# Attention and a gated feed-forward on one core: the value product on 128 rows in every pass, and the statistics of q and k in a PSUM bank of VectorE's own

## The chip, the core and the metric

The kernel runs on one core of a Trainium2 chip. The core has five engines with their own instruction streams: TensorE (PE in the profile; PEld is its weight load), VectorE (DVE), ScalarE (ACT), GpSimd (POOL) and SyncE (SP, here only a DMA queue). On-chip memory is SBUF (128 partitions, read and written by all engines and by DMA) and PSUM (8 banks of 128 x 512 float32), into which TensorE writes. The metric is the device time of one execution in microseconds (us), as the median of some runs; lower is better.

## The reference

```python
def rmsnorm(x, g):
    return x / np.sqrt(np.mean(x * x, axis=-1, keepdims=True) + 1e-06) * g
# q, k, v: 8 batches, 12 heads, 448 tokens, 64 features, float32
q_n, k_n = rmsnorm(q, g_q), rmsnorm(k, g_k)
scores = (1.0 / np.sqrt(64)) * np.matmul(q_n, k_n.transpose(0, 1, 3, 2))
attn = softmax(scores)                     # with 1e-09 added to the sum
x = np.matmul(attn, v)                     # -> [8, 448, 768]
x_prev = x shifted by one token
xk = mu_k * x + (1.0 - mu_k) * x_prev
xr = mu_r * x + (1.0 - mu_r) * x_prev
k = np.maximum(xk @ w_k, 0.0)              # 768 -> 1024; the weights are float64
out = sigmoid(xr @ w_r) * (k * k @ w_v)    # 1024 -> 768
```

## The kernel before

Every float32 product is made of float16 parts: a value is split into a high and a low half ("hi", "lo"), and three products (hi hi, hi lo, lo hi) are added up in PSUM.

Attention goes over 48 **pairs** of heads (`i`), and its inputs over 24 **quads** of heads (`u`, two pairs each).

- `prep(u)` normalises k and q of a quad. ScalarE squares (`xs`), GpSimd adds halves of the squares (L167), VectorE sums them (L170) into 28 numbers a partition, two short VectorE instructions scale them (L172, L173), and `rsqrt` (L64) takes the reciprocal root by a bit trick (L67, L68) and three Newton steps of three instructions each (L70, L71, L72). All of it lies in SBUF: the statistics and the root in a tile `ss` of 56 columns, the scratch in a tile that the profile calls `rs`. GpSimd multiplies q and k by the root (L179), ScalarE and GpSimd split them (L184, L186), and DMA transposes on SyncE's queue put them into `stk`.
- `vprep(i)` scales v of a pair. Each row's sum of squares is spread over the partitions by a small matmul (L204) into a PSUM tile `tr`, VectorE takes its maximum (L206) and makes a power of two of it (L208 to L210), ScalarE writes the high half `vh` (L211), VectorE the low half `vl` (L215).
- `group_scores` makes scores of 64 to 128 query rows (TensorE, L235), their maxima (VectorE, L258) and their exponentials in place in PSUM (ScalarE, L259). `group_probs` divides by the sum (L271, L272), splits the result (ScalarE L277, VectorE L278: tile `ph`), and a DMA transpose on SyncE's queue makes `pT`.
- `attend(i)` multiplies `pT` with `vh` and `vl` in 11 passes over the same PSUM tile `av`, two matmuls (one per head) in a pass. A pass takes 128 rows of `pT`; ten of them use all, and the eighth, `(1, 3, HD)`, only the first 64, so that its matmuls have the tile shape 64*64 on the array where the others have 128*64. ScalarE then scales `av` into `x` (L303).

`weight_tile` turns the float64 weights into scaled float16 halves in 20 tiles: VectorE assembles float32 (L404 to L406, two rounds a tile), six or eight matmuls write a Gram matrix into the PSUM tile `av` (L412), VectorE multiplies it by the identity (L416), a matmul sums it (L417), VectorE takes the maximum (L418). `moe(b)` is the feed-forward of a batch, with its matmuls at L456 into the PSUM tile `mm`.

The eight PSUM banks are: `sc` four, `mm` two, `av` one (attention's value product and the weights' Gram matrices by turns), `tr` one (`vprep` and the one call of `allmax`). A tile with one buffer is given to its next user when the last one's reader is done; the users have the order in which the code asks for it.

The three streams (attention, weights, feed-forward) are interleaved by the loop at the end of the kernel, and a scheduler then sets the order in which each engine's instructions stand. Each engine works its instructions off in that order and stands still when the first of them waits.

Of the kernel before, what the change touches and what calls it, by code (L numbers as in the profile page):

```python
# [7 lines left out]
F32 = mybir.dt.float32  # L8
F16 = mybir.dt.float16
BF16 = mybir.dt.bfloat16  # L10
I32 = mybir.dt.int32
AF = mybir.ActivationFunctionType
ALU = mybir.AluOpType
AX = mybir.AxisListType

P = 128
HD = 64
NT = 7
# [36 lines left out]
def spread(ap, n):  # L55
    return bass.AP(tensor=ap.tensor, offset=ap.offset, ap=[list(x) for x in ap.ap] + [[0, n]])
# [4 lines left out]
    return bass.AP(tensor=ap.tensor, offset=ap.offset + off, ap=[list(ap.ap[0]), [HD, 2], [2 * HD, NT], [1, HD]])  # L61


def rsqrt(nc, pool, y, a, n, tag):  # L64
    t = pool.tile([P, n], F32, name=tag)
    yi = y.bitcast(I32)
    nc.vector.tensor_scalar(out=yi, in0=a.bitcast(I32), scalar1=1, scalar2=None, op0=ALU.logical_shift_right)  # L67
    nc.vector.tensor_scalar(out=yi, in0=yi, scalar1=-1.0, scalar2=float(0x5F3759DF), op0=ALU.mult, op1=ALU.add)  # L68
    for _ in range(NEWTON):
        nc.vector.tensor_tensor(out=t, in0=y, in1=y, op=ALU.mult)  # L70
        nc.vector.scalar_tensor_tensor(out=t, in0=t, scalar=-0.5, in1=a, op0=ALU.mult, op1=ALU.mult)  # L71
        nc.vector.scalar_tensor_tensor(out=y, in0=t, scalar=1.5, in1=y, op0=ALU.add, op1=ALU.mult)  # L72


def attn_moe_kernel(tc, q, k, v, g_q, g_k, mu_k, mu_r, w_k, w_v, w_r, out):
    nc = tc.nc
# [11 lines left out]
    ident16 = const.tile([P, P], BF16, name="ident16")  # L88
    nc.scalar.copy(out=ident16, in_=ident)

    def allmax(src, n, r):
        pt = ps.tile([P, 512], F32, name="tr", bufs=1)
        nc.tensor.transpose(out=pt[0:n, 0:P], in_=src, identity=ident)
        m = small.tile([P, 1], F32, name="allmax")
        nc.vector.tensor_reduce(out=m[0:n, :], in_=pt[0:n, 0:P], axis=AX.X, op=ALU.max)
        nc.tensor.matmul(out=pt[:, P:P + n], lhsT=m[0:n, :].broadcast_to([n, P]), rhs=ident[0:n, 0:n], start=True, stop=True)
        nc.vector.tensor_copy(out=r, in_=pt[:, P:P + n])
# [13 lines left out]
    gm = const.tile([P, 8], F32, name="gm")  # L111
    nc.vector.tensor_reduce(out=gm[:, 0:1], in_=G, axis=AX.X, op=ALU.max, apply_absolute_value=True)
    nc.vector.tensor_scalar(out=gm[:, 0:1], in0=gm[:, 0:1], scalar1=TINY, scalar2=None, op0=ALU.max)
    rsqrt(nc, small, gm[:, 1:2], gm[:, 0:1], 1, "rs1")
    nc.vector.tensor_scalar(out=G, in0=G, scalar1=gm[:, 1:2], scalar2=None, op0=ALU.mult)
    nc.vector.tensor_tensor(out=gm[:, 2:3], in0=gm[:, 1:2], in1=gm[:, 1:2], op=ALU.mult)
    nc.vector.tensor_scalar(out=gm[:, 3:4], in0=gm[:, 2:3], scalar1=1.0 / HD, scalar2=None, op0=ALU.mult)
# [21 lines left out]
    NSS = 4 * NT  # L139
# [19 lines left out]
        VF[i] = vf  # L159

    def prep(u):
        ss = small.tile([P, 2 * NSS], F32, name="ss", bufs=2)
        for n, t in enumerate(LD[u]):
            tv = t.rearrange("p h (t d) -> p (h t) d", d=HD)
            xs = ap_.tile([P, 2 * NT, HD], F32, name="xs", bufs=1)
            nc.scalar.activation(out=xs, in_=tv, func=AF.Square)  # L166
            nc.gpsimd.tensor_tensor(out=xs[:, :, 0:HD // 2], in0=xs[:, :, 0:HD // 2], in1=xs[:, :, HD // 2:], op=ALU.add)  # L167
            if n == 0:
                nc.gpsimd.tensor_tensor(out=tv, in0=tv, in1=bcast(G[:, :], 2 * NT), op=ALU.mult)  # L169
            nc.vector.tensor_reduce(out=ss[:, 2 * NT * n:2 * NT * (n + 1)], in_=xs[:, :, 0:HD // 2], axis=AX.X, op=ALU.add)  # L170
            yield
        nc.vector.tensor_scalar(out=ss[:, 0:2 * NT], in0=ss[:, 0:2 * NT], scalar1=1.0 / HD, scalar2=1e-6, op0=ALU.mult, op1=ALU.add)  # L172
        nc.vector.tensor_scalar(out=ss[:, 2 * NT:NSS], in0=ss[:, 2 * NT:NSS], scalar1=gm[:, 3:4], scalar2=gm[:, 4:5], op0=ALU.mult, op1=ALU.add)  # L173
        rsqrt(nc, small, ss[:, NSS:2 * NSS], ss[:, 0:NSS], NSS, "rs28")
        yield
        T = [ap_.tile([P, 2, 2 * NT, HD], F16, name="stk", bufs=3) for x in range(2)]
        for n, t in enumerate(LD.pop(u)):
            tv = t.rearrange("p h (t d) -> p (h t) d", d=HD)
            nc.gpsimd.tensor_tensor(out=tv, in0=tv, in1=spread(ss[:, NSS + 2 * NT * n:NSS + 2 * NT * (n + 1)], HD), op=ALU.mult)  # L179
            pool = pro[0] if u < NP // 2 and n else ap_  # L180
            nat = pool.tile([P, 2 * NT, P], F16, name="nat", bufs=1)
            hi, lo = heads(nat, 0), heads(nat, NT * P)
            t4 = t.rearrange("p h (t d) -> p h t d", d=HD)
            nc.scalar.copy(out=hi, in_=t4)  # L184
            yield
            nc.gpsimd.tensor_tensor(out=lo, in0=t4, in1=hi, op=ALU.subtract)  # L186
            for x in range(2):
                nc.sync.dma_start_transpose(out=T[x][:, n], in_=nat[x * HD:(x + 1) * HD].rearrange("p a c -> p (a c)"))
            yield
        for x in range(2):  # L190
            TQ[2 * u + x] = T[x]

    def vprep(i):
# [5 lines left out]
        vh = ap_.tile([P, 2, NT, HD], F16, name="vh", bufs=2)  # L199
        vl = ap_.tile([P, 2, 4, HD], F16, name="vl", bufs=2)  # L200
        vs = small.tile([P, 2], F32, name="vs", bufs=2)
        pt = ps.tile([P, 512], F32, name="tr", bufs=1)
        nc.scalar.activation(out=vh[0:HD].rearrange("p h t d -> p h (t d)").bitcast(BF16), in_=vf[0:HD], func=AF.Square, accum_out=vs[0:HD, 0:1])
        nc.tensor.matmul(out=pt[:, 0:HD], lhsT=vs[0:HD, 0:1].bitcast(BF16)[:, 1:2].broadcast_to([HD, P]), rhs=ident16[0:HD, 0:HD], start=True, stop=True)  # L204
        yield
# [78 lines left out]
                nc.sync.dma_start_transpose(out=pT[:, h, :, t0 * HD:], in_=ph[h * HD:(h + 1) * HD, 0, :])  # L284
        yield

    PASSES = [(hl, c, P) for c in range(3) for hl in range(2)] + [(0, 3, P), (1, 3, HD)] + [(0, c, P) for c in range(4, 7)]

    def attend(i):
        vh, vl, iv = VV.pop(i)  # L290
# [319 lines left out]
```

## Time and profile before

| | us |
|---|---|
| median of 3 runs (lowest, highest) | 1267.06 (1266.27, 1267.16) |
| the profiled execution, its own time | 1263.01 |
| span of its instructions | 1261.2 |
| TensorE matmul busy | 1017.4 |
| VectorE busy | 901.4 |
| ScalarE busy | 794.4 |
| GpSimd busy | 681.4 |
| mean granted TensorE clock | 0.911 |

Busy time is the union of an engine's instructions. A line of the page names the source line, the engine, the operation, the tile written and those read (`ss<-rs,ss`), the shapes, the count, and then busy time in us and the mean of one in ns. Where a tile's or a line's instructions are listed, the three numbers are the shortest, median and longest duration in ns. A view of windows gives each engine's busy time in a stretch of the span, with the number of instructions. A view of waits says which engine's instruction stood idle until which other one, with the sum in us, the number of times and the longest.

The span has three stages: up to about 400 us the weights are prepared beside the first twelve or so pairs; up to 1174 us attention and feed-forward run beside each other; then the rest of the feed-forward runs alone.

### The profile page before, as it was taken

The page shows a single profiled execution, that of the slowest core. Times are in us where ns is not written, and L with a number is a line of the kernel's source. Part 1 is how long each engine was busy: PE and PEld are TensorE (multiplying, and loading weights), DVE is VectorE, ACT ScalarE, POOL GpSimd, SP SyncE. Part 2 cuts the span into 40 slices and gives each one's busy share as a digit, 9 for nine tenths or more (in the row PEclk, how much of TensorE's full clock was granted, in tenths as well). Part 3 has the DMA queues.
Part 4 walks back from the last instruction along what each step waited for, and adds up shares of the span by engine and source line. Part 5 has one row for each costly group of instructions (what it writes and reads, how often), then busy time and mean ns, then how long its engine had stood idle before and what let it go on. Part 6 is the DMA issues. An engine that isn't in the chain of part 4 may idle for free. (4 is left out here: it accounts for less than half of the span.)

```text
span 1261.2 us, 18897 instructions
## 1 busy us (share of the span) xinstructions
PE 1017.4 (81%) x5935; PEld 471.4 (37%) x5935; DVE 901.4 (71%) x2356; ACT 794.4 (63%) x1756; POOL 681.4 (54%) x678
## 2 busy tenths in 40 slices
PE   1125545586799999889999899898989999999998
PEld 0002222233244344433443444344434444344454
DVE  5886899979967868675786667776887687667200
ACT  3266656566756777577676765776778676876311
POOL 2642465736655657375467536674568455523731
PEclk9956656588799999998999999999989999999999
DMA  7589977978586878768777676978986787776101
GB/s 161 119 152 168 178 155 160 172 153 165 110 148 134 146 145 167 139 131 142 143 147 147 128 138 138 167 132 152 167 162 129 151 150 125 136 144 102 26 13 38
DMA packets 456356, 172.77 MB, mean 137 GB/s; under 512 B 411200, under 2 KB 452672, under 8 KB 456256
## 3 DMA queue, kind: packets, MB, share of 16 engines
q1 hardware_dynamic: 423328, 132.24, 59.2%
q10 hardware_dynamic: 32928, 39.34, 12.8%
q8 instruction: 46, 0.75, 0.2%
q14 instruction: 54, 0.44, 0.1%
HBM read 61.41 MB, written 11.01 MB: 57 GB/s over the span
## 5 line engine op out<-in xcount | busy, mean ns | idle before, releaser
L278 DVE SCALAR_TENSOR_TENSOR ph<-sc,sums,ph 128x448 f16<-128x448 f32 x322 | 210.0, 676 | 87.8 <-ACT ph L277 87.2
L259 ACT ACTIVATE sc<-sc,sums 128x448 f32<-128x448 f32 x322 | 193.3, 612 | 108.8 <-DVE sums L258 91.5
L235 PE MATMUL sc<-stk 64*128 64x448 f16 (+1 forms) x1104 | 189.9, 379 | 68.1 <-DVE ph L278 49.7
L456 PE MATMUL mm<-wvh,kk 128*128 128x384 f16 x896 | 234.6, 330 | 0.1
L456 PE MATMUL mm<-xk,wkh 128*128 128x448 f16 x768 | 220.9, 366 | 12.7 <-ACT kf L478 6.0
L277 ACT ACTIVATE ph<-sc,sums 128x448 f16<-128x448 f32 x322 | 189.6, 645 | 50.3 <-DMA pT<-ph 15.7
L258 DVE TENSOR_REDUCE sums<-sc 128x1 f32<-128x448 f32 x322 | 187.8, 613 | 22.8 <-PE sc L235 22.3
L456 PE MATMUL mm<-wrh,xr 128*128 128x384 f16 x672 | 178.4, 329 | 6.9 <-ACT th L512 4.7
L235 PE MATMUL av<-pT,vh 128*64 128x448 f16 x672 | 142.0, 389 | 40.8 <-DMA pT<-ph 26.0
L456 PEld LDWEIGHTS <-kk 128*128 128x128 f16 x1344 | 125.8, 98 | 101.0 <-issue 25.3
L456 PE MATMUL mm<-wvl,kk 128*128 128x384 f16 x448 | 147.5, 329 | 0.0
L456 PE MATMUL mm<-xk,wkl 128*128 128x448 f16 x384 | 140.6, 366 | 0.0
L186 POOL TENSOR_TENSOR nat<-qk,nat 128x896 f16<-128x896 f32 x48 | 91.2, 1900 | 74.4 <-ACT nat L184 74.3
L167 POOL TENSOR_TENSOR xs<-xs 128x448 f32<-128x448 f32 x48 | 56.2, 1172 | 138.1 <-ACT xs L166 138.0
L235 PEld LDWEIGHTS <-stk 64*128 64x128 f16 (+1 forms) x1152 | 57.6, 101 | 193.5 <-issue 142.3
L456 PEld LDWEIGHTS <-xr 128*128 128x128 f16 x1008 | 93.1, 98 | 85.1 <-issue 23.6
L373 DVE SCALAR_TENSOR_TENSOR df<-x,bsc,df 128x448 f32<-128x448 f32 x90 | 90.7, 1018 | 35.8 <-POOL df L372 35.6
L179 POOL TENSOR_TENSOR qk<-qk,ss 128x896 f32<-128x896 f32 x48 | 82.0, 1728 | 60.2 <-DVE ss L72 49.2
L456 PE MATMUL mm<-wrl,xr 128*128 128x384 f16 x336 | 110.5, 329 | 0.0
L456 PEld LDWEIGHTS <-wkh 128*128 128x128 f16 x768 | 72.8, 100 | 92.8 <-issue 39.0
L516 POOL TENSOR_TENSOR o<-th,bsc 128x384 f32<-128x384 f32 x48 | 43.2, 899 | 104.8 <-DVE th L515 68.1
L166 ACT ACTIVATE xs<-qk 128x896 f32<-128x896 f32 x48 | 45.8, 954 | 79.3 <-DMA qk<-in_q_dram 50.8
(124 smaller groups left out, 1722.2 us busy)
## 6 DMA issues: line engine op xcount, KB each, us to landing
vf<-in_v_dram SPq DMA_DIRECT2D x48, 224.0 KB, 3.8
qk<-in_k_dram ACTq DMA_DIRECT2D x48, 224.0 KB, 4.9
qk<-in_q_dram ACTq DMA_DIRECT2D x48, 224.0 KB, 4.8
out_dram<-o SPq DMA_DIRECT2D x56, 192.0 KB, 2.9
vf<-in_v_dram SPq DMA_DIRECT2D x48, 192.0 KB, 3.8
raw<-in_moe_w_k_dram ACTq DMA_DIRECT2D x16, 384.0 KB, 3.9
raw<-in_moe_w_v_dram ACTq DMA_DIRECT2D x12, 512.0 KB, 4.7
raw<-in_moe_w_r_dram ACTq DMA_DIRECT2D x12, 384.0 KB, 4.5
```

The source lines that it names most:

```text
L166: nc.scalar.activation(out=xs, in_=tv, func=AF.Square)
L167: nc.gpsimd.tensor_tensor(out=xs[:, :, 0:HD // 2], in0=xs[:, :, 0:HD // 2], in1=xs[:, :, HD // 2:], op=ALU.add)
L179: nc.gpsimd.tensor_tensor(out=tv, in0=tv, in1=spread(ss[:, NSS + 2 * NT * n:NSS + 2 * NT * (n + 1)], HD), op=ALU.mult)
L186: nc.gpsimd.tensor_tensor(out=lo, in0=t4, in1=hi, op=ALU.subtract)
L235: return op(**kw)
L258: nc.vector.tensor_reduce(out=sums[:, t:t + 1], in_=sp[:, 0:S], axis=AX.X, op=ALU.max, negate=True)
L259: nc.scalar.activation(out=sp[:, 0:S], in_=sp[:, 0:S], func=AF.Exp, bias=sums[:, t:t + 1], accum_out=sp[:, S:S + 1])
L277: nc.scalar.activation(out=ph[:, j, 0:S], in_=sp[:, 0:S], func=AF.Copy, scale=r[:, j:j + 1])
L278: nc.vector.scalar_tensor_tensor(out=ph[:, j, S:], in0=sp[:, 0:S], scalar=r[:, j:j + 1], in1=ph[:, j, 0:S], op0=ALU.mult, op1=ALU.subtract)
L373: nc.vector.scalar_tensor_tensor(out=df, in0=xc, scalar=sc[:, MX + j:MX + j + 1], in1=df, op0=ALU.mult, op1=ALU.add)
L456: nc.tensor.matmul(out=ps_, lhsT=la(i, a), rhs=ra(i, c), start=(i == 0 and a + c == 0), stop=(i == n - 1 and a == 1))
L516: nc.gpsimd.tensor_tensor(out=o[:, hs].rearrange("p (c n) -> p c n", n=P), in0=th.rearrange("p (c n) -> p c n", n=P), in1=spread(rsu[:, ND ...
```

## The change

It has two parts, and one that follows from the second.

1. In `PASSES` the eighth pass takes all 128 rows: `(1, 3, P)`. The second 64 rows add, for every seventh token, the low half of its probabilities times the low half of its values, a term that was left out before. All 22 matmuls of a pair now have the shape 128*64.
2. A PSUM tile `misc` is allotted once for the whole program. The statistics of q and k and the scratch of `rsqrt` lie in it, in 56 columns for even quads and 56 for odd ones, and only VectorE touches it. The root itself stays in SBUF (tile `ss`, now 28 columns), since GpSimd reads it. `rsqrt` is rewritten so that each of its instructions with two tensors takes one from `misc` and one from SBUF; it has as many instructions as before. In the setup one copy of a column into `misc` is added.
3. `misc` takes the bank of `tr`, so the PSUM tile of `vprep` and of `allmax` becomes a user of the bank `av`.

```diff
-def rsqrt(nc, pool, y, a, n, tag):
-    t = pool.tile([P, n], F32, name=tag)
-    yi = y.bitcast(I32)
-    nc.vector.tensor_scalar(out=yi, in0=a.bitcast(I32), scalar1=1, scalar2=None, op0=ALU.logical_shift_right)
-    nc.vector.tensor_scalar(out=yi, in0=yi, scalar1=-1.0, scalar2=float(0x5F3759DF), op0=ALU.mult, op1=ALU.add)
+def rsqrt(nc, y, a, t):
+    ti = t.bitcast(I32)
+    nc.vector.tensor_scalar(out=ti, in0=a.bitcast(I32), scalar1=1, scalar2=None, op0=ALU.logical_shift_right)
+    nc.vector.tensor_scalar(out=y.bitcast(I32), in0=ti, scalar1=-1.0, scalar2=float(0x5F3759DF), op0=ALU.mult, op1=ALU.add)
     for _ in range(NEWTON):
-        nc.vector.tensor_tensor(out=t, in0=y, in1=y, op=ALU.mult)
-        nc.vector.scalar_tensor_tensor(out=t, in0=t, scalar=-0.5, in1=a, op0=ALU.mult, op1=ALU.mult)
+        nc.vector.tensor_tensor(out=t, in0=a, in1=y, op=ALU.mult)
+        nc.vector.scalar_tensor_tensor(out=t, in0=t, scalar=-0.5, in1=y, op0=ALU.mult, op1=ALU.mult)
         nc.vector.scalar_tensor_tensor(out=y, in0=t, scalar=1.5, in1=y, op0=ALU.add, op1=ALU.mult)
...
+    misc = ps.tile([P, 512], F32, name="misc", bufs=1)
+
     def allmax(src, n, r):
-        pt = ps.tile([P, 512], F32, name="tr", bufs=1)
+        pt = ps.tile([P, 512], F32, name="av", bufs=1)
...
-    rsqrt(nc, small, gm[:, 1:2], gm[:, 0:1], 1, "rs1")
+    nc.vector.tensor_copy(out=misc[:, 510:511], in_=gm[:, 0:1])
+    rsqrt(nc, gm[:, 1:2], misc[:, 510:511], misc[:, 511:512])
...
     def prep(u):
-        ss = small.tile([P, 2 * NSS], F32, name="ss", bufs=2)
+        y = small.tile([P, NSS], F32, name="ss", bufs=2)
+        o = (u % 2) * 2 * NSS
+        ss, tm = misc[:, o:o + NSS], misc[:, o + NSS:o + 2 * NSS]
...
-        rsqrt(nc, small, ss[:, NSS:2 * NSS], ss[:, 0:NSS], NSS, "rs28")
+        rsqrt(nc, y, ss, tm)
...
-            nc.gpsimd.tensor_tensor(out=tv, in0=tv, in1=spread(ss[:, NSS + 2 * NT * n:NSS + 2 * NT * (n + 1)], HD), op=ALU.mult)
+            nc.gpsimd.tensor_tensor(out=tv, in0=tv, in1=spread(y[:, 2 * NT * n:2 * NT * (n + 1)], HD), op=ALU.mult)
...
     def vprep(i):
-        pt = ps.tile([P, 512], F32, name="tr", bufs=1)
+        pt = ps.tile([P, 512], F32, name="av", bufs=1)
...
-    PASSES = [(hl, c, P) for c in range(3) for hl in range(2)] + [(0, 3, P), (1, 3, HD)] + [(0, c, P) for c in range(4, 7)]
+    PASSES = [(hl, c, P) for c in range(3) for hl in range(2)] + [(0, 3, P), (1, 3, P)] + [(0, c, P) for c in range(4, 7)]
```

The kernel's line numbers grow by one to four below the first of these lines; L67 to L72 of before are L66 to L71 after, L204 is L208, L412 is L416, L417 is L421.

The scheduler's order changes in many small places on every engine; the numbers of instructions stay, but for the one copy on VectorE. Two places show what matters. The first is VectorE in `prep` of one quad: what its instructions of the reciprocal root write and read (the first Newton step and its start). Before:

```order
L173 TENSOR_SCALAR ss<-ss,gm 128x14 [waits DVE_49]
L67 TENSOR_SCALAR ss<-ss 128x28 [waits DVE_49]
L68 TENSOR_SCALAR ss<-ss 128x28 [waits DVE_49]
L70 TENSOR_TENSOR rs_3281<-ss 128x28 [waits DVE_49]
L71 SCALAR_TENSOR_TENSOR rs_3281<-rs_3281,ss 128x28 [waits DVE_49]
L72 SCALAR_TENSOR_TENSOR ss<-rs_3281,ss 128x28 [waits DVE_49]
```

After (other instructions of VectorE stand between some of these, in both):

```order
L177 TENSOR_SCALAR misc<-misc,gm 128x14 [waits DVE_49]
L66 TENSOR_SCALAR misc<-misc 128x28 [waits DVE_49]
L67 TENSOR_SCALAR ss<-misc 128x28 [waits DVE_49]
L69 TENSOR_TENSOR misc<-misc,ss 128x28 [waits DVE_49]
L70 SCALAR_TENSOR_TENSOR misc<-misc,ss 128x28 [waits DVE_49]
L71 SCALAR_TENSOR_TENSOR ss<-misc,ss 128x28 [waits DVE_49]
```

All of them still wait only for VectorE itself; of the two tensors that one reads, one now is in PSUM (`misc`).

The second is TensorE among the weights: the matmul of `vprep` (`vs` is its stationary input) beside the Gram matrices (`wf`) and their sum (`dg`) of the fourth and fifth weight tile. Before, it has a bank of its own and stands ahead of the sum, with nothing to wait for but its input:

```order
L235 LDWEIGHTS stk [waits DMAHW1_49,DMAHW3_49]
L235 MATMUL sc<-stk 128x448 [waits DVE_49]
L204 LDWEIGHTS vs [waits Activation_49]
L204 MATMUL tr<-ident_75,vs 128x64
L417 MATMUL av<-dg,ones 128x128 [waits DVE_49]
L412 LDWEIGHTS wf
L412 MATMUL av<-wf 128x128 [waits DVE_49]
```

After, it stands between the sum of one tile and the Gram matrix of the next:

```order
L421 MATMUL av<-dg,ones 128x128 [waits DVE_49]
L208 LDWEIGHTS vs [waits Activation_49]
L208 MATMUL av<-ident_75,vs 128x64 [waits DVE_49]
L416 LDWEIGHTS wf
L416 MATMUL av<-wf 128x128 [waits DVE_49]
```

It moved behind the sum, now waits for VectorE to have read that sum, and the next Gram matrix waits for VectorE to have read its result.

## The prediction

> **What bounds the kernel now.** I read the windows of the three stages first, then what TensorE and VectorE wait for in each, then the rows of the instructions that change.
>
> Busy times of the three stages (stretch, its length, then busy time and count of PE, PEld, DVE, ACT, POOL; clock, DMA share, GB/s):
>
> ```profile
> 0.00:400.00 400.00, 217.94 (x1164) 96.11 (x1165) 326.29 (x846) 232.18 (x479) 206.87 (x182) 0.76 0.79 152
> 400.00:1174.00 774.00, 719.52 (x4308) 329.89 (x4305) 563.07 (x1495) 541.21 (x1230) 439.42 (x458) 0.98 0.76 142
> 1174.00:1261.20 87.20, 79.90 (x467) 45.39 (x465) 12.07 (x15) 21.03 (x48) 35.08 (x39) 0.98 0.07 19
> ```
>
> The first 400 us are VectorE's: it is busy for 82% of them (326 of 400), TensorE for 54%. In the next 774 us TensorE is busy for 93% (54.5 us idle) and VectorE for 73%. The last 87 us are feed-forward alone, nearly all TensorE. A microsecond saved is thus worth most on VectorE in the first stage and on TensorE in the second.
>
> TensorE's waits, from 0 to 400 us:
>
> ```profile
> PE av L412 <- DVE wf L406: 40.4, 12, 7.8
> PE sc L235 <- DVE ph L278: 32.0, 11, 15.2
> ...
> PE av L235 <- DVE WSC L418: 6.2, 4, 3.4
> PE av L412 <- DVE WSC L418: 6.1, 3, 3.4
> ```
>
> From 400 to 1174 us:
>
> ```profile
> PE av L235 <- DMA pT<-ph: 26.0, 22, 3.0
> PE sc L235 <- DVE ph L278: 17.7, 18, 2.5
> ```
>
> And VectorE's own longest there:
>
> ```profile
> DVE ph L278 <- ACT ph L277: 69.6, 63, 4.2
> ```
>
> Early on TensorE waits for VectorE by name; later its idle time goes first to the transposes of the probabilities, then to VectorE (17.7 us), and VectorE itself waits for ScalarE. So what VectorE gains later reaches the end only in part.
>
> **The short instructions of `prep` (term 1).** These are the instructions on the tile `ss` (shortest, median and longest in ns), then their busy time by stage:
>
> ```profile
> L70 DVE TENSOR_TENSOR rs<-ss x72: 160/186/962, 27.5 to 1049.3; 128x28 f32<-128x28 f32 x72
> L71 DVE SCALAR_TENSOR_TENSOR rs<-rs,ss x72: 160/183/1114, 28.3 to 1050.5; 128x28 f32<-128x28 f32 x72
> L72 DVE SCALAR_TENSOR_TENSOR ss<-rs,ss x72: 161/186/1828, 29.4 to 1050.7; 128x28 f32<-128x28 f32 x72
> L170 DVE TENSOR_REDUCE ss<-xs x48: 599/608/621, 13.3 to 1045.6; 128x14 f32<-128x448 f32 x48
> ...
> L172 DVE TENSOR_SCALAR ss<-ss x24: 158/724/1695, 14.2 to 1031.4; 128x14 f32<-128x14 f32 x24
> L173 DVE TENSOR_SCALAR ss<-ss,gm x24: 280/294/1251, 23.5 to 1047.3; 128x14 f32<-128x14 f32 x24
> L67 DVE TENSOR_SCALAR ss<-ss x24: 153/175/2066, 24.2 to 1047.6; 128x28 int32<-128x28 int32 x24
> L68 DVE TENSOR_SCALAR ss<-ss x24: 160/180/1657, 24.4 to 1047.8; 128x28 int32<-128x28 int32 x24
> ```
>
> ```profile
> 0.00:400.00 400.00, 54.20 (x135) 31.97 (x18) 0.76 0.79 152
> 400.00:1174.00 774.00, 79.38 (x225) 49.98 (x30) 0.98 0.76 142
> ```
>
> The same work takes 160 ns or, in its worst case, 1.8 us. L170, which reads one tensor of SBUF, never stretches. The same split shows in VectorE's large instructions:
>
> ```profile
> L278 DVE SCALAR_TENSOR_TENSOR ph<-sc,sums,ph x322: 656/675/686, 77.7 to 1163.7; 128x448 f16<-128x448 f32 x161
> ```
>
> ```profile
> L416 DVE TENSOR_TENSOR dg<-av,ident x20: 274/278/292, 27.6 to 314.3; 128x128 f32<-128x128 f32 x20
> ```
>
> ```profile
> L373 DVE SCALAR_TENSOR_TENSOR df<-x,bsc,df x90: 666/716/2297, 257.1 to 1195.8; 128x448 f32<-128x448 f32 x90
> ```
>
> L278 and L416 read one tensor from PSUM and one from SBUF, the form that `rsqrt` gets, and never stretch in 342 executions; L373, with both in SBUF, goes up to 2297 ns. I read this as VectorE waiting for GpSimd at something that both need for a second SBUF operand. [...]
>
> The clean price of one `prep`: three Newton steps at the shortest 160 + 160 + 161 ns, plus 158 + 280 + 153 + 160 ns, plus two L170 at 608: 3.41 us. With the medians in place of the shortest (L172 but kept at 158): 3.69 us. Nine of the 24 lie before 400 us (135 instructions, 15 each). So the stretching costs 54.2 - 9 x 3.41 = 23.5 us (21.0 by medians) there, and 79.4 - 15 x 3.41 = 28.2 us (24.0) later. I take 22 and 26 us of VectorE's time.
>
> What of it reaches the end: in the first stage at most VectorE's busy share, 0.82, since it is the engine waited for; at least 0.2, if waits for loads hold the stage as well (DMA share 0.79). I take half: 11 us. In the second stage TensorE's whole idle time in VectorE's name is 17.7 us of the 54.5, so I take a quarter: 6.5 us (ends 0 and half, 13).
>
> **What PSUM costs instead.** For reading, a reduction of 64 columns from PSUM and one from SBUF:
>
> ```profile
> L206 DVE TENSOR_REDUCE vs<-tr x48: 205/215/226, 14.1 to 1140.4; 128x1 f32<-128x64 f32 x48
> ```
>
> ```profile
> L112 DVE TENSOR_REDUCE gm<-gq x1: 221/221/221, 6.5 to 6.5; 128x1 f32<-128x64 f32 x1
> ```
>
> They cost the same, and L278's shortest (656) is that of L373 (666). I take nothing. Upper end: L416 at 128 columns takes 92 ns more than L70's median at 28, and if a column cost nothing all of it would be PSUM's. For writing, VectorE has no row; ScalarE's are next:
>
> ```profile
> L259 ACT ACTIVATE sc<-sc,sums 128x448 f32<-128x448 f32 x322 | 193.3, 612 | 108.8 <-DVE sums L258 91.5
> ...
> L277 ACT ACTIVATE ph<-sc,sums 128x448 f16<-128x448 f32 x322 | 189.6, 645 | 50.3 <-DMA pT<-ph 15.7
> ```
>
> Writing to PSUM was 33 ns shorter than to SBUF. I take 0, with 33 ns either way on 11 instructions of each `prep`: 11 x 24 x 33 ns = 8.7 us of VectorE, about 3 us at the shares above. The copy in the setup costs one short instruction, some 0.16 us at L70's price, covered by the first loads.
>
> **The eighth pass (term 2).** One value product in TensorE's order of time (start, length, then the form; x2 is both heads side by side):
>
> ```profile
> 704.69 0.36 PE L235 MATMUL av<-pT,vh 128*64 128x448 f16 x2
> 704.88 0.35 PE L235 MATMUL av<-pT,vl 128*64 128x448 f16 x2
> 705.06 0.35 PE L235 MATMUL av<-pT,vh 128*64 128x448 f16 x2
> 705.35 0.38 PE L235 MATMUL av<-pT,vl 64*64 64x448 f16 x2
> 705.66 0.76 PE L235 MATMUL av<-pT,vh 128*64 128x448 f16 x5
> ```
>
> Passes start 0.19 us apart, but 0.29 and 0.31 us into and out of the pass of shape 64*64. The step costs 0.10 + 0.12 = 0.22 us a pair. With one shape I expect 0.19 us throughout: pass length goes by 448 columns, not rows (the 64-row pass is no shorter). 48 pairs at 0.21 us are 10.1 us of TensorE. Twelve pairs lie before 400 us, at TensorE's busy share of 0.54: 1.4 us. The other 36, at 0.93: 7.0 us. Together 8.4 us. Ends: 0 if the step turns up elsewhere, 10.6 if all counts.
>
> **The bank that is shared now (term 3).** Among the weights, up to about 315 us, ten matmuls of `vprep` stand between uses of `av`. In the new order eight are followed at once by a Gram matrix, and four come at most two matmuls after a tile's sum: 12 crossings at which TensorE waits until VectorE has read the bank, with the next scores queued behind. The rows on `WSC` above are that wait: 12.3 us in seven, 1.76 us each. 12 x 1.76 = 21.1 us of TensorE standing. TensorE is idle for 46% of that stage anyway, and much of it at the same places (40.4 us for `wf`), so I take a fifth: 4 us; ends 0 and 21.1. Later at least 17 matmuls, of attention and feed-forward, lie between it and a value product on either side, and I price it at nothing; what covers it is this distance, and without it each pair would pay about the 1.76 us.
>
> **Sum.** -11 - 6.5 - 8.4 + 4 = -21.9 us. Against the profiled execution's 1263.01 us that is 1241.1. The median of the runs shown is 4.05 us above it (1267.06), so I forecast 1245.
>
> **Rivals**, as medians:
>
> - VectorE's stretching was hidden: TensorE has other work, and VectorE then waits longer for ScalarE (the 69.6 us row). Terms 2 and 3 remain: -4.4, 1262.7.
> - VectorE sets the pace: shares 0.82 and 0.5 give -18 - 13 - 8.4 + 4 = -35.4, 1231.7. The first windows row speaks for it, the DMA share of 0.79 against.
> - A PSUM operand is dear: 13 instructions of each `prep` read one. At 92 ns that is 10.8 us in the nine early ones and 17.9 us in the others; at my shares +5.4 + 4.5 = +9.9: 1255. L206 beside L112 speaks against. [...]
> - The end grows: after the last value product the new order has 504 feed-forward matmuls, the old one 465. At the last window's 79.90 us for 467, 39 more are +6.7 us, if attention does not end earlier for it: 1252.
> - The shared bank decides: at the longest wait seen, 3.4 us, 12 crossings on the path of the scores cost 40.8 us in the first 315 us: -25.9 + 40.8 = +14.9, 1282. It turns the sign from 2.16 us a crossing (25.9 / 12), if all lie on the path.
> - The change doesn't do what it says: the instructions stretch on, since the root stays in SBUF, and only terms 2 and 3 are left, half of term 2 with them: 1267.
>
> **How the numbers follow.** Forecast 0.48, hidden 0.14, pace 0.13, dear PSUM 0.06, longer end 0.08, bank 0.07, no effect 0.04. About 0.2% (2.5 us) is what a measurement of this kernel can tell from no change. The first, third, fourth and fifth are faster, and so is half or a little more of "hidden" (0.08 of its 0.14, 0.05 same, 0.01 slower); the bank is slower, "no effect" half same, half slower. That makes faster 0.83, same 0.07, slower 0.10. The range goes from 1226 (pace, with its last shares a little higher) to 1264 (hidden, with its bank cost a little higher), and leaves out the bank, "no effect" and the far tails.
>
> **What would show it.** Right: the lines of L70 to L72 with medians near 160 to 190 and longest times under 300 ns, VectorE's busy sum about 48 us less; no `av` matmul of shape 64*64 and no start 0.3 us late within a value product; the window to 400 us shorter by about 8 us net. Wrong: waits of `av` on `vs` or `WSC` of 20 us or more; short instructions on `misc` at 220 ns or more; as much idle time of TensorE as before while VectorE's sum has fallen.

## The result, and the profile after

The changed kernel takes 1222.37 us (median of 4 runs, 1221.22 to 1226.41), the kernel before 1266.66 us on the same chip: a ratio of 0.9673 [0.964, 0.9705], 44 us less where 22 were forecast. The profiled execution took 1221.22 us, its span is 1219.4 us, its mean granted clock 0.917 (0.911 before).

The three stages again (stretch, length, busy time and count of PE, PEld, DVE, ACT, POOL; clock, DMA share, GB/s):

```profile
0.00:400.00 400.00, 239.48 (x1302) 108.35 (x1302) 336.08 (x911) 256.75 (x531) 232.81 (x206) 0.79 0.84 164
400.00:1174.00 774.00, 727.83 (x4393) 342.03 (x4394) 521.87 (x1441) 533.67 (x1208) 449.05 (x467) 0.98 0.76 137
1174.00:1219.40 45.40, 39.59 (x244) 23.61 (x242) 3.32 (x6) 5.31 (x18) 5.18 (x7) 0.98 0.14 35
```

In the first 400 us every engine did more work than before: TensorE 239.5 us (217.9), ScalarE 256.8 (232.2), GpSimd 232.8 (206.9). That stage did not only get rid of some VectorE time, it ran more densely. How far attention has come is read from the rows in which ScalarE scales a finished pair (first, thirteenth and forty-sixth in order of time). Before, then after:

```profile
108.79 0.64 ACT L303 ACTIVATE x<-av,bstat 128x448 f32<-128x448 f32 x1
...
410.03 0.63 ACT L303 ACTIVATE x<-av,bstat 128x448 f32<-128x448 f32 x1
...
1135.30 0.64 ACT L303 ACTIVATE x<-av,bstat 128x448 f32<-128x448 f32 x1
```

```profile
89.38 0.63 ACT L307 ACTIVATE x<-av,bstat 128x448 f32<-128x448 f32 x1
...
385.55 0.63 ACT L307 ACTIVATE x<-av,bstat 128x448 f32<-128x448 f32 x1
...
1093.10 0.66 ACT L307 ACTIVATE x<-av,bstat 128x448 f32<-128x448 f32 x1
```

By these rows the lead is 19.4 us at the first pair, 24.5 at the thirteenth and 42.2 at the forty-sixth; at the end of the span it is 41.8. The first of these figures says too much. TensorE's last value product of the first pair, before and then after:

```profile
98.05 0.76 PE L235 MATMUL av<-pT,vh 128*64 128x448 f16 x6
```

```profile
88.35 0.38 PE L239 MATMUL av<-pT,vh 128*64 128x448 f16 x1
```

They end at 98.8 and 88.7 us, 10.1 us apart. The other 9 us come from ScalarE, whose order before puts three products of probabilities (L277) ahead of the scaling. By the last value products the lead is 10.1 us at the first pair, 23.2 at the second, 13.3 at the fourth and 24.6 at the thirteenth. So a quarter of the gain is there at the first pair, when three of 24 `prep` have run, and it goes up and down before it grows.

The instructions on `misc` (shortest, median, longest in ns):

```profile
L69 DVE TENSOR_TENSOR misc<-misc,ss x72: 171/184/196, 28.5 to 1009.3; 128x28 f32<-128x28 f32 x72
L70 DVE SCALAR_TENSOR_TENSOR misc<-misc,ss x72: 172/185/196, 29.1 to 1010.9; 128x28 f32<-128x28 f32 x72
L71 DVE SCALAR_TENSOR_TENSOR ss<-misc,ss x72: 166/178/188, 29.4 to 1012.2; 128x28 f32<-128x28 f32 x72
L174 DVE TENSOR_REDUCE misc<-xs x48: 607/618/629, 13.5 to 1004.1; 128x14 f32<-128x448 f32 x48
```

No Newton step stretches any more (longest 196 ns, 1828 before), and PSUM costs next to nothing at 28 columns: medians of 184, 185 and 178 ns against 186, 183 and 186, shortest times of 171, 172 and 166 against 160, 160 and 161. What they waited for before is in the trace: GpSimd. Of the 312 instructions of 14 or 28 columns (all of `prep` but L170), 72 took over 200 ns (L173: over 300); each of the 72 ran beside GpSimd for at least 85% of its time and ended within 0.05 us of the end of a GpSimd instruction, as here:

```profile
35.62 3.08 POOL L169 TENSOR_TENSOR qk<-qk,gq 128x896 f32<-128x896 f32 x1
```

```profile
36.66 2.07 DVE L67 TENSOR_SCALAR ss<-ss 128x28 int32<-128x28 int32 x1
```

In the changed kernel 127 of the 312 ran beside a GpSimd instruction, and none stretched. The 15 instructions of all `prep` take 89.4 us, added up, against 133.6 in the two window rows of before: 44 us less. VectorE's whole busy time fell by 40 us, not by the 48 of the forecast:

```profile
PE 1006.9 (83%) x5935; PEld 474.0 (39%) x5935; DVE 861.3 (71%) x2357; ACT 795.7 (65%) x1756; POOL 687.0 (56%) x678
```

Some of it came back among the weights. In the groups by line (busy us, mean ns) these are L405 and L406 of before, which read two tensors in SBUF, and the same lines after:

```profile
L405 DVE SCALAR_TENSOR_TENSOR wf<-raw,wf 128x384 int32<-128x384 int32 (+1 forms) x40 | 34.4, 865 | 0.1
L406 DVE SCALAR_TENSOR_TENSOR wf<-raw,wf 128x384 int32<-128x384 int32 (+1 forms) x40 | 33.5, 837 | 0.2
```

```profile
L409 DVE SCALAR_TENSOR_TENSOR wf<-raw,wf 128x384 int32<-128x384 int32 (+1 forms) x40 | 40.4, 1012 | 0.1
L410 DVE SCALAR_TENSOR_TENSOR wf<-raw,wf 128x384 int32<-128x384 int32 (+1 forms) x40 | 38.9, 973 | 0.1
```

They take 11.4 us more. The run with `misc` in SBUF and this order (below) has 75.9 us for the two, so 8.0 us of it come with the order and 3.4 with the place.

The eighth pass is gone as a form (one line for all 384 products with `vl`), and after 400 us (clock 0.98) passes start 0.19 us apart in the median, those around the former eighth one too:

```profile
L239 PE MATMUL av<-pT,vl x384: 350/353/583, 83.7 to 1126.8; 128*64 128x448 f16 x192
```

```profile
733.80 0.54 PE L239 MATMUL av<-pT,vh 128*64 128x448 f16 x2
733.99 0.54 PE L239 MATMUL av<-pT,vl 128*64 128x448 f16 x2
734.18 0.54 PE L239 MATMUL av<-pT,vh 128*64 128x448 f16 x2
734.37 0.54 PE L239 MATMUL av<-pT,vl 128*64 128x448 f16 x2
734.56 0.54 PE L239 MATMUL av<-pT,vh 128*64 128x448 f16 x2
```

TensorE's waits up to 400 us, and then from 400 to 1174 us:

```profile
PE sc L239 <- DVE ph L282: 25.0, 17, 13.3
PE av L416 <- DVE wf L410: 23.4, 6, 7.6
...
PE av L416 <- DVE vs L210: 7.4, 5, 2.5
```

```profile
PE av L239 <- DMA pT<-ph: 16.7, 13, 2.9
PE sc L239 <- DVE ph L282: 13.3, 12, 3.2
```

The wait for `wf` fell from 40.4 to 23.4 us, that for `ph` from 32.0 to 25.0, later that for the transposes from 26.0 to 16.7. The shared bank shows as a wait on `vs` of 7.4 us in five.

What the eighth pass cost before is more than the one product in the prediction shows. A usual product:

```profile
1026.50 0.51 PE L235 MATMUL av<-pT,vh 128*64 128x448 f16 x2
1026.94 0.38 PE L235 MATMUL av<-pT,vl 64*64 64x448 f16 x2
1027.24 0.38 PE L235 MATMUL av<-pT,vh 128*64 128x448 f16 x2
```

Over the 30 products after 400 us in which nothing came between, the median from the start of the pass before it to the start of the pass behind it was 0.775 us, and 0.378 in the kernel with all 128 rows: 0.40 us a pair, not 0.21.

### The profile page after: what moved, and what is told of

It is laid out like the page before. It is cut to its first block, busy times and chain, and to the rows that moved or that the text cites. A ratio compares the mean times of both kernels' runs of the same rounds, so it can differ in the third digit from the quotient of the medians.

```text
span 1219.4 us, 18884 instructions
## 1 busy us (share of the span) xinstructions
PE 1006.9 (83%) x5935; PEld 474.0 (39%) x5935; DVE 861.3 (71%) x2357; ACT 795.7 (65%) x1756; POOL 687.0 (56%) x678
## 5 line engine op out<-in xcount | busy, mean ns | idle before, releaser
L263 ACT ACTIVATE sc<-sc,sums 128x448 f32<-128x448 f32 x322 | 193.8, 610 | 109.3 <-DVE sums L262 98.5
L239 PE MATMUL sc<-stk 64*128 64x448 f16 (+1 forms) x1104 | 194.8, 384 | 49.7 <-DVE ph L282 38.3
L239 PE MATMUL av<-pT,vh 128*64 128x448 f16 x672 | 138.4, 386 | 26.5 <-DMA pT<-ph 21.8
L460 PE MATMUL mm<-xk,wkl 128*128 128x448 f16 x384 | 138.0, 359 | 0.0
L275 DVE TENSOR_SCALAR sums<-sc 128x1 f32<-128x1 f32 x322 | 46.6, 150 | 81.8 <-ACT sc L263 80.2
L377 DVE SCALAR_TENSOR_TENSOR df<-x,bsc,df 128x448 f32<-128x448 f32 x90 | 86.0, 963 | 25.9 <-POOL df L376 25.6
L170 ACT ACTIVATE xs<-qk 128x896 f32<-128x896 f32 x48 | 45.7, 952 | 81.8 <-DMA qk<-in_q_dram 38.6
```

The lines of the kernel that those rows point to most:

```text
L239: return op(**kw)
L263: nc.scalar.activation(out=sp[:, 0:S], in_=sp[:, 0:S], func=AF.Exp, bias=sums[:, t:t + 1], accum_out=sp[:, S:S + 1])
L275: nc.vector.tensor_scalar(out=r[:, j:j + 1], in0=sp[:, S:S + 1], scalar1=1e-9, scalar2=2.0 ** -15, op0=ALU.add, op1=ALU.mult)
L377: nc.vector.scalar_tensor_tensor(out=df, in0=xc, scalar=sc[:, MX + j:MX + j + 1], in1=df, op0=ALU.mult, op1=ALU.add)
L460: nc.tensor.matmul(out=ps_, lhsT=la(i, a), rhs=ra(i, c), start=(i == 0 and a + c == 0), stop=(i == n - 1 and a == 1))
```

## The experiments

Three causes were in the change: the place of `misc`, the eighth pass, the bank. A fourth came with them: the order in which the scheduler puts each engine's instructions, which it works out anew for every program and which can come out another one. Theory A: the stretching was worth nearly its full VectorE time. Rival C: the new order did it. Where an experiment is "held to an order", one line is added at the end of the kernel that chains each engine's instructions in the order of a table, without any wait:

```diff
+    in_order(tc, nc)    # every instruction of an engine after the one before it in the table
     ctx.close()
```

**The parts one by one, in the scheduler's own order.** The kernel before with the eighth pass alone:

```diff
-    PASSES = [...] + [(0, 3, P), (1, 3, HD)] + [...]
+    PASSES = [...] + [(0, 3, P), (1, 3, P)] + [...]
```

> The kernel before with the eighth pass on 128 rows and nothing else. The change as a whole gained 44 us of 1267, where the prediction gave 22. Theory A (VectorE's stretching in prep was worth most of it, about 33 us, and the pass what its 0.21 us a pair say): 9 us less than before, about 1258. Rival B (the pass is worth more, since the value product lies on attention's chain): 20 us less or more, 1247 or below. Rival C (the new order of instructions is a lucky one, and each part has its forecast price): 8 us less, but up to 10 us either way, since this kernel's order is another one again.

Measured: 1261.73 us, ratio 0.9993 [0.997, 1.0015]: nothing that can be told from zero. The trace shows that the order did not change here: every engine has its instructions, and ScalarE and SyncE their DMA issues, in the places of before. So theory C's ten microseconds either way had no ground in this run.

The changed kernel without it (that line put back):

> The changed kernel with the eighth pass back on 64 rows (that term of the product is left out again): statistics and scratch in the PSUM bank, and the shared bank, alone. A: 33 us less than before, about 1233. B: 22 us less at most, 1245 or above. C: 13 to 18 us less, 1249 to 1254, with 10 us either way.

Measured: 1215.93 us, 0.9637 [0.9602, 0.9672], less than any of the three theories had it. The whole gain is in the PSUM bank, or comes with it.

The changed kernel with `misc` in SBUF, one line:

```diff
-    misc = ps.tile([P, 512], F32, name="misc", bufs=1)
+    misc = const.tile([P, 512], F32, name="misc")
```

> The changed kernel with the tile misc in SBUF: same instructions, same shared bank, same passes, but each of rsqrt's two-tensor instructions reads both from SBUF again. All theories: the instructions on misc stretch to 1 us and more again. A: about 33 to 37 us more than the changed kernel, 1255 to 1260. C: half of that, 1240, because the stretching itself was worth 17 us.

Measured: 1266.78 us, 1.0037 [1.0011, 1.0062]. All of the gain is gone, more than either theory allowed. But so is the order: of VectorE's 2357 instructions in the trace 548 stand in the same place as in the changed kernel, and TensorE ends the first pair's products at 100.3 us, as late as before (98.8).

The kernel before with the bank alone (`vprep` and `allmax` in `av`, one bank unused):

```diff
-        pt = ps.tile([P, 512], F32, name="tr", bufs=1)
+        pt = ps.tile([P, 512], F32, name="av", bufs=1)
```

> The kernel before with the PSUM tile of vprep and allmax in the bank of the value product, and nothing else (the eighth bank stays empty). The prediction's price of the shared bank: 4 us more than before, about 1271, ends 1267 and 1288. If the shared bank brought a better order (C): up to 10 us less than before.

Measured: 1259.26 us, 0.9966 [0.9938, 0.9994]. In the order that it got, sharing the bank does not cost, though TensorE's waits on `vs` and `WSC` for that bank rose from 12.3 to 26.9 us. What it costs in one and the same order was not measured.

**Place and order apart.** `misc` in SBUF, every engine held to the changed kernel's order:

```diff
-    misc = ps.tile([P, 512], F32, name="misc", bufs=1)
+    misc = const.tile([P, 512], F32, name="misc")
+ORDER = (the changed kernel's order of all five engines)
```

> The changed kernel with the tile misc in SBUF, as in the run before, but every engine's instructions are held to the order of the changed kernel, so that only the place of misc differs from it. Theory A (the stretching itself costs nearly its full time): about 1262, some 40 us more than the changed kernel's 1222. Rival C (the scheduler's other order made the gain): about 1240, of the 44 us some 17.

Measured: 1248.36 us, 0.9863 [0.9812, 0.9914], between the two theories. The trace has all 2357 VectorE instructions in the places of the changed kernel, and those of the other engines too. The instructions stretch as before, and VectorE is busy for 31 us more than in the changed kernel:

```profile
L69 DVE TENSOR_TENSOR misc<-misc,ss x72: 163/182/1558, 28.5 to 1033.7; 128x28 f32<-128x28 f32 x72
```

```profile
PE 1007.8 (81%) x5935; PEld 474.3 (38%) x5935; DVE 892.0 (72%) x2357; ACT 796.3 (64%) x1756; POOL 685.6 (55%) x678
```

`misc` in PSUM, TensorE, ScalarE, GpSimd and SyncE held to the order of the kernel with `misc` in SBUF (VectorE free):

```diff
+ORDER = (four engines' order in the kernel with misc in SBUF)
```

> The other way round: misc in PSUM, and TensorE, ScalarE, GpSimd and the DMA queue held to the order that the scheduler gave the version with misc in SBUF (1266.8 us); VectorE's order is left to the scheduler. A: the gain stays, 1222 to 1230. C: it goes with the order, 1245 to 1260.

Measured: 1254.23 us, 0.9913 [0.9886, 0.994]. No stretching (longest 196 ns), 33.5 us less VectorE time than with `misc` in SBUF, but 12.6 us less in the end by the medians, and the first pair's products end at 98.6 us again. VectorE, left free, got another order: 1236 of its 2357 instructions stand in the same place as with `misc` in SBUF. So both theories hold a part, and neither has the whole. As ratios to before on the same chip, at 1265 us: the new order alone gives 22 us (1.0037 to 0.9863), clean instructions alone 16 (1.0037 to 0.9913), both together 46 (1.0037 to 0.9673).

These steps start from the order of the kernel with `misc` in SBUF, which is not the order of before. From before itself the way is this: the pass alone, in the order of before, 1 to 5 us (0.9993 above, 0.9963 below); the new order, with the shared bank and the rewritten `rsqrt` in it, 13 us (0.9963 to 0.9863, both on one chip; uncertain by 7); the place of `misc`, with every engine's order held, 24 us (0.9863 to 0.9673; uncertain by 8).

**Where the order pays.** The order was then changed in two pieces, up to the last value product of the first pair ("prologue") and behind it ("rest"); P is the changed kernel's, S that of the kernel with `misc` in SBUF. Three kernels, the first with `misc` in SBUF:

```diff
+ORDER = (prologue P, rest S; five engines)
```

> The changed kernel with the misc tile in SBUF again. Every engine is held to an order: up to the last value product of pair 0 that of the changed kernel (95 matmuls, 182 instructions of VectorE, 89 of ScalarE, 29 of GpSimd, 23 issues of SyncE), behind it that of the kernel with misc in SBUF and the scheduler's own order (1266.8 us; the same with the whole of the changed kernel's order: 1248.4 us). Theory P, the order pays in the prologue alone: pair 0 ends near 95 us and not near 110.6, and the time is 1249 to 1252 us. Rival, the order of the steady part pays too, or the lead is lost again: 1257 to 1267 us, with pair 0 near 95 us all the same.

Measured: 1252.16 us, 0.9904 [0.9872, 0.9935].

```diff
+ORDER = (prologue S, rest P; four engines, VectorE free)
```

> The changed kernel (misc in PSUM), TensorE, ScalarE, GpSimd and SyncE held to an order, VectorE free: up to the last value product of pair 0 that of the kernel with misc in SBUF in the scheduler's own order, behind it that of the changed kernel. Theory P, the order pays in the prologue alone: pair 0 ends near 110 us and not near 90, and the time is 1238 to 1244 us (1222.4 plus some 20), most of the way to the 1254.2 us with the whole of that order. Rival, the steady part's order carries it: 1222 to 1230 us.

Measured: 1237.99 us, 0.9777 [0.9755, 0.98].

```diff
+ORDER = (prologue P, rest S; four engines, VectorE free)
```

> The changed kernel (misc in PSUM), TensorE, ScalarE, GpSimd and SyncE held to an order, VectorE free: up to the last value product of pair 0 that of the changed kernel, behind it that of the kernel with misc in SBUF in the scheduler's own order. The eighth cell of place of misc, order of the prologue, order of the rest. If the prologue's worth (15 us with the changed kernel's rest, 15 us with misc in SBUF) is its own: 1254.2 less 15, 1236 to 1242 us, and then the rest's order is worth 14 to 20 us with misc in PSUM and 4 us with misc in SBUF. If the lead lives on only where the rest's order fits it: 1246 to 1256 us.

Measured: 1245.39 us, 0.9856 [0.9829, 0.9883], between what the two theories expected. In the first two the time came at the edge of what theory P says (1249 to 1252 and 1238 to 1244 us), but the first pair did not end where it says. The row of the first finished pair in these three kernels, in the order above:

```profile
100.67 0.68 ACT L323 ACTIVATE x<-av,bstat 128x448 f32<-128x448 f32 x1
```

```profile
98.73 0.67 ACT L323 ACTIVATE x<-av,bstat 128x448 f32<-128x448 f32 x1
```

```profile
96.69 0.68 ACT L323 ACTIVATE x<-av,bstat 128x448 f32<-128x448 f32 x1
```

Here too the row depends on what ScalarE's order puts ahead of the scaling. The last value products tell the prologue better. With prologue S they end at 100.3 us in SBUF and at 98.6 and 98.5 in PSUM; with prologue P at 93.5 and 93.8 in SBUF and at 88.9 and 88.7 in PSUM. The prologue's order brings the first pair forward by 7 us in SBUF and 10 in PSUM, and clean instructions by 2 us in S and 5 in P.

The cells as ratios to the kernel before on the same chip (in the upper three with PSUM VectorE's order is free):

| prologue, rest | `misc` in SBUF | `misc` in PSUM |
|---|---|---|
| S, S | 1.0037 | 0.9913 |
| P, S | 0.9904 | 0.9856 |
| S, P | not run | 0.9777 |
| P, P | 0.9863 | 0.9673 |

At 1265 us a step of 0.001 is 1.27 us. The place of `misc` is worth 16 us in order S, 6 in the mixed one, 24 in order P. The prologue's order is worth 17 us in SBUF, 7 (rest S) and 13 (rest P) in PSUM; the rest's order 5 us in SBUF, but 17 and 23 in PSUM. Each ratio is uncertain by 0.002 to 0.005, which is 3 to 6 us, and a difference of two differences by some 9. Only in order P is the place of `misc` tested with all five engines held: in the other two rows VectorE's order differs between the columns (1236 and 1373 of 2357 places are the same). That place and order are worth more together (16 and 24 us, 8 apart) is therefore not shown; the 18 us between 6 and 24 go beyond the noise, but may come from VectorE's order. Two waits of TensorE over the whole span show place and order at work. `misc` in SBUF, order S:

```profile
PE sc L239 <- DVE ph L282: 60.8, 27, 15.3
PE av L239 <- DMA pT<-ph: 35.4, 22, 5.6
```

`misc` in PSUM, order S:

```profile
PE sc L255 <- DVE ph L298: 53.2, 20, 15.8
PE av L255 <- DMA pT<-ph: 34.6, 22, 5.5
```

`misc` in SBUF, order P:

```profile
PE sc L255 <- DVE ph L298: 53.3, 33, 18.1
PE av L255 <- DMA pT<-ph: 22.3, 17, 5.3
```

The changed kernel:

```profile
PE sc L239 <- DVE ph L282: 38.3, 29, 13.3
PE av L239 <- DMA pT<-ph: 21.8, 17, 4.3
```

The wait for the transposes goes by the order (35 to 22 us) and not by the place. The wait for VectorE's `ph` falls by 7.6 us with clean instructions in order S, and by 15.0 in order P.

**What in the prologue's order?** Before, ScalarE reaches the first heads' float16 casts (L184) only after two weight loads that hold it, and GpSimd's subtractions stand behind other work. Those four instructions were moved ahead, the rest held to the order of before:

```diff
 ScalarE, in order
-L399 raw x2, L184 nat, L403 wf, L184 nat
+L184 nat, L184 nat, L399 raw x2, L403 wf
 GpSimd, in order
-L423 wf, L179 qk x2 (next heads), L186 nat x2
+L186 nat x2, L423 wf, L179 qk x2 (next heads)
```

> The kernel before, held to its own order but for two moves in the prologue: the two float16 casts (L184) of the first four heads stand on ScalarE ahead of the two raw-weight loads (L399) that held it until 45.2 us, and GpSimd's two subtractions (L186) that follow them stand ahead of its weight scaling (L423) and the scaling (L179) of the next four heads. Theory Q, the order's gain in the prologue is these two blocked queues: the first scores start at 51 to 54 us and not at 59.8, pair 0 ends 6 to 8 us earlier than 109.4, and the time falls by 4 to 8 us. Rival, the next four heads are then late instead (they were ready at 61.7 us and come some 4 us later): the first scores are early, pair 0 ends within 2 us of 109.4, and the time stays.

Measured: 1266.25 us, 1.0017 [0.9994, 1.004], as the rival has it; the first pair ends at 107.0 us, its last value product at 97.6 (98.8 before, 88.7 in the changed kernel). The first scores start at 52.7 us instead of 59.8, and then wait for VectorE, which stands at a weight tile until ScalarE has copied it (L420 is L404 of before, L274 is L258):

```profile
61.05 0.95 DVE L420 TENSOR_SCALAR wf<-wf 128x384 int32<-128x384 int32 x1 [5.03 <-ACT wf L419]
...
64.57 0.61 DVE L274 TENSOR_REDUCE sums<-sc 128x1 f32<-128x448 f32 x1
```

So the row maxima, exponentials and first products were moved ahead of that too:

```diff
 VectorE, in order
-L404 x2, L405 x2, L258, L406, L258, L406, L271, L258, L170, L258, L271, L173, L271, L258, L272
+L258 x2, L271, L258 x2, L271 x2, L258, L272, L404 x2, L405 x2, L406 x2, L170, L173
 ScalarE, in order
-L403 x2, L166, L184, L259, L399, L259, L399, L259, L166, L403, L259, L403, L259, L277 x2
+L259 x5, L277 x2, L403 x2, L166, L184, L399 x2, L166, L403 x2
```

> As the run that moved the four float16 casts and subtractions first, and beside it: on VectorE the first row maxima and sums of pair 0 (the first L258, L271, L272 rows) stand ahead of the next six operations on raw weights (L404 to L406), which had held VectorE until 64.6 us for a ScalarE result (L403), and on ScalarE the first five exponentials (L259) and two products (L277) stand ahead of the two L403 and of two loads. Theory Q, the prologue's gain is the scores of pair 0 no longer standing behind weight work on two in-order engines: the first maxima at 54 to 58 us (64.6), the first product of VectorE (L278) at 68 to 72 us (76.0), pair 0 ends at 97 to 102 us (107.0), and the time is 6 to 12 us under before. Rival, weight work put off comes due within the first pairs and takes the lead back: pair 0 early, the time within 4 us of before.

Measured: 1265.18 us, 1.0017 [0.9997, 1.0038]: no gain, and no early first pair either; it ends at 110.1 us, its last value product at 99.4. The maxima come at 55.8 us, but the exponentials only at 60.7, behind ScalarE's loads, and the six weight operations, put off, now stand ahead of VectorE's first `ph` (here L294), at 78.8 us, later than the 77.7 of before:

```profile
55.77 1.14 DVE L274 TENSOR_REDUCE sums<-sc 128x1 f32<-128x448 f32 x2
61.38 0.16 DVE L287 TENSOR_SCALAR sums<-sc 128x1 f32<-128x1 f32 x1 [4.47 <-ACT sc L275]
...
67.40 3.63 DVE L422 SCALAR_TENSOR_TENSOR wf<-raw,wf 128x384 int32<-128x384 int32 x2
...
78.79 0.68 DVE L294 SCALAR_TENSOR_TENSOR ph<-sc,sums,ph 128x448 f16<-128x448 f32 x1
```

The wait moved one place on in the same queue each time. The prologue's gain is thus not in these rows by themselves; which set of rows is enough stays open.

**The eighth pass with the order held.** The kernel before with that pass, held to the order of before:

```diff
-    PASSES = [...] + [(0, 3, P), (1, 3, HD)] + [...]
+    PASSES = [...] + [(0, 3, P), (1, 3, P)] + [...]
+ORDER = (that of before, five engines)
```

> The kernel before with the eighth pass on 128 rows, held to the order of the kernel before on every engine. TensorE issues 10 us less. If that time is on the path (prediction's term 2) and the other order of the pass alone hid it: 8 us less than before. If attention's chain on VectorE and ScalarE sets the end and TensorE only waits longer: 0, within 3 us.

Measured: 1260.34 us, 0.9963 [0.9935, 0.999]: 4.7 us. Its order is the same as that of the run with the pass alone (0.9993), so the two measure the same thing; taken together they give 2.4 us, uncertain by 2.2. TensorE had more to gain than was forecast: in the 41 products in which nothing came between the passes, these two runs start the pass behind the eighth one 13.8 and 12.7 us earlier, added up. A fifth of that reaches the end. The other way round, the changed kernel in its own order with three passes of 64 rows:

```diff
-    PASSES = [(hl, c, P) for c in range(3) for hl in range(2)] + [(0, 3, P), (1, 3, P)] + [(0, c, P) for c in range(4, 7)]
+    PASSES = [(hl, c, HD if hl and c != 1 else P) for c in range(4) for hl in range(2)] + [(0, c, P) for c in range(4, 7)]
```

> The changed kernel in its own order, with three passes of the low half on 64 rows (their second 64 rows of the product are left out), each between passes on 128 rows: six changes of shape a pair more than in the changed kernel, at 0.10 us each 0.6 us a pair and 30 us of TensorE in all. If TensorE's time is on the path: 25 us more than the changed kernel, about 1247. If attention's chain sets the end: 0 to 8 us more, 1222 to 1230.

Measured: 1239.51 us, 0.9797 [0.9745, 0.985]: 16 us more than the changed kernel. Each change of shape costs about a tenth of a microsecond here, as the forecast had it (0.29 to 0.31 us between starts, against 0.19):

```profile
738.75 0.36 PE L255 MATMUL av<-pT,vl 128*64 128x448 f16 x2
738.94 0.35 PE L255 MATMUL av<-pT,vh 128*64 128x448 f16 x2
739.23 0.38 PE L255 MATMUL av<-pT,vl 64*64 64x448 f16 x2
739.54 0.38 PE L255 MATMUL av<-pT,vh 128*64 128x448 f16 x2
```

Six more in each of 48 pairs at 0.11 us are 32 us, of which half reaches the end (16 us, uncertain by 8), where the two theories had nearly all and at most a quarter. Why the one short pass of before cost more than two such changes stays open.

**The best of them.** The changed kernel, all passes on 128 rows, held to the order of the kernel with the PSUM bank alone:

```diff
+ORDER = (that of the changed kernel with its eighth pass on 64 rows, five engines)
```

> The changed kernel, all 128 rows in its eighth pass, held to the order that the scheduler chose for the kernel with the PSUM bank alone (1215.9 us with the eighth pass on 64 rows). If the eighth pass is worth its 5 us with the order held, as in the order of the kernel before, 1209 to 1212 us; if passes pay only where they change what the scheduler does, 1215 to 1217 us.

Measured: 1215.6 us, 0.9591 [0.9569, 0.9613], the fastest ratio of all, below the changed kernel's interval. Against 0.9637 [0.9602, 0.9672] for the same order with the short pass, the pass is worth 6 us by the ratios, with an uncertainty of 5; the medians (1215.6 and 1215.93) show none of it. So the median falls where the second expectation has it, and the ratio leaves room for the first.

## Why the prediction was off

- **The step that failed** is the sum's silence on the order. The text on the change says that it moves "in many small places on every engine", and then prices only one consequence, a longer end among the rivals (it came, and did not count: what stands behind the last value product took 91.7 us where it had taken 87.1, but that product ended 46.4 us earlier). Everything else was read off the trace of before as if each wait would stay where it was. Between two orders, with every instruction stretching as before, lie 22 us (`misc` in SBUF). Counted from before, the new order with the shared bank in it is worth 13 us, where the sum has +4 for the bank and nothing for the order. These 17 us are most of the 22 that were missing; the place of `misc` brought 6 more than forecast, the pass 3 to 7 less. Which places in the order pay was not found, and nothing in the trace of before says that the scheduler would come upon a better order: that it did is luck.
- **Term 1** (stretching, -17.5) lies inside what was measured for the place of `misc` alone in one order: 24 us, uncertain by 8. Its mechanism held to the row: operands in PSUM, no stretching, 196 ns at the longest among the Newton steps. Its reading that a second SBUF operand makes an instruction stretch is too narrow: L67, L68 and L172 read one SBUF tensor and took up to 2066 ns. Two sizes in it were off against each other. VectorE's busy time fell by 31 us where the order was the same, not by 48. And more of it counted than a half early and a quarter later: 24 of 31 us.
- **PSUM at no cost** was right: the rival of 92 ns is out for short instructions whose first operand is in PSUM: here L69 takes 184 ns in the median (171 at the shortest), L70 of before 186 (160).
- **Term 2** (the eighth pass, -8.4) has both of its factors off. One product was taken for all, 0.21 us a pair where the median is 0.40; and the share of 0.83 is far too high: the two runs with this pass alone give 2.4 us of at least 13.
- **Term 3** (the bank, +4) is not seen: 0.9966 for the bank alone, 4 us less and not more, but in an order of its own. The crossings are there: the waits of `av` on `vs` and `WSC` add up to 20.0 us (12.3 before), as much as was named as a sign of being wrong, and in the run with the bank alone to 26.9. That they fall where TensorE was idle anyway is likely, and not shown. The rival by which they would decide is out.
- The rival "VectorE sets the pace" (1231.7) came nearest in time; it too lacks the order.
- Of the signs named ahead, the clean medians, the absent shape and the absent long starts came; VectorE's sum fell by 40 us and not 48; the window to 400 us was to shorten by 8 us and did by 24.5 at the thirteenth pair, far more than the early terms of the sum give.

## What to carry to other kernels

Where a scheduler sets the order, a change has two effects, what its instructions cost and what order the scheduler makes of it; hold the order fixed in one run and the instructions fixed in another, and price both before the sum is believed. Count from the order that the kernel had, too: here 13 us from before, 22 from another order of the same scheduler. Choose the row that marks progress with care: the first pair's lead was 19 us by ScalarE's row and 10 by TensorE's, since an order can put other work ahead of either. And compare traces instruction by instruction before a run is called another order: two runs that were to differ in it had the same one.

## What the runs showed of the hardware

- Short VectorE instructions on SBUF stretched beside GpSimd: of the 312 of before 93 ran beside a GpSimd instruction, and 72 of these stretched, to as much as 2066 ns; all 72 ended with a GpSimd instruction. With the tile in PSUM 127 ran beside one, and none of 312 went over 299 ns.
- TensorE writes into PSUM alone in these traces (all 5935 matmuls write `sc`, `mm`, `av` or `tr`), though the introduction has SBUF as written by all engines.
- Stretching that was taken off some VectorE instructions went in part to others: in the same order of instructions those of `prep` were 35.8 us shorter with `misc` in PSUM (125.2 to 89.4 us, added up) and VectorE's busy time only 30.7 (892.0 to 861.3), and the three operations on raw weights 5.8 us longer (104.3 to 110.1). The Newton steps took up to 1582 ns there with `misc` in SBUF, up to 196 ns with it in PSUM.
- Executions of one and the same kernel spread by 0.8% (17 runs of before, 1258.87 to 1269.29 us), and one and the same program, run on two chips, came out at 0.9993 and 0.9963 of before. Over these 17 the mean granted clock (0.911 to 0.935) does not go with it: its correlation with the time is -0.03, where 25 runs of before on another chip gave -0.49 (0.909 to 0.934).
